# A decode kernel's first load ahead of its opening barrier, a semaphore barrier at its end, w_o of 28 heads in one transfer, and its output gathered to one partition

## Chip, cores and metric

The kernel runs on one core of a Trainium2 chip. The metric is the device time of one execution in microseconds (us). For every execution two numbers are recorded: this time, and the span, which goes from the first to the last instruction that the profile shows. For the difference of the two I write "time minus span". The record marks as fast every execution for which it lists a state, at mean granted TensorE clocks of 0.770 to 0.792.

## The reference, cut to what matters

One token is decoded (batch 1, width 512): layer norm, grouped-query attention with 32 query heads over 8 cached heads of 65536 keys each, output projection, residual, layer norm, a gated MLP of width 1792, residual. The two caches in bf16 are 268 of the 282 MB that are read.

```python
x = A_x
h = x + _A_ref(_layernorm(x), A_k_cache, A_v_cache, A_wq, A_wo)
#   softmax(q k^T * Dh**-0.5) v, then @ wo; q = (x @ wq), 32 heads of 128
h2 = h + _B_ref(_layernorm(h), B_w_gate, B_w_up, B_w_down)
#   (sigmoid(x @ w_gate) * (x @ w_up)) @ w_down
```

## The kernel before: the parts that matter here

The kernel streams the caches through a ring of four 4 MB slots with large transfers that SyncE (SP) issues. DVE transposes K, TensorE (PE) makes scores and value products. The program is five instruction streams, one for each engine, inside a block whose entry and exit are barriers of all engines:

```python
WO = ((0, 16), (16, 8), (24, 4), (28, 4))     # w_o: pieces of 16, 8, 4, 4 heads
WD_SPLIT = [(0, 7), (7, 12), (12, 14)]        # w_down: rows in three pieces
...
V_SPLIT = [(0, 3), (3, 4)]                    # the last V block in two pieces
W_SPLIT = {"wg": [(0, 4)], "wu": [(0, 3), (3, 4)]}
...
def regroup(i):                               # brings the heads' outputs into w_o's row order
    j0, n = WO[i]
    ...                                       # DVE product -> Lw[i]
    op("pe", lambda e: e.matmul(ps(OT[i], 0, n), lhsT=Lw[i][:, :], rhs=row_of[n][:, :], start=True, stop=True), ...)
    op("dve", lambda e: e.tensor_copy(O3[:, j0:j0 + n], ps(OT[i], 0, n)), ...)
...
for i, (nm, bank) in enumerate((("wg", GB), ("wu", UB))):
    ...                                       # 16 products for gate, 16 for up
    if i == 0:                                # the fp32 residual product, between the two
        op("pe", lambda e: e.matmul(ps(YB, 0, 128), lhsT=gsel[:, :], rhs=hz[:, :], start=True, stop=False, ...), ["hz"])
...                                           # tanh on ACT, product and transpose on DVE, 56 w_down products on PE
op("dve", lambda e: e.tensor_copy(y_sb[:, :], ps(YB, 0, 128)), ["y"], "ysb")
dma("sp", lambda e: e.dma_start(out[0].rearrange("o (g n) -> (o g) n", g=4),
                                bass.AP(tensor=y_sb, offset=0, ap=[[32 * 128, 4], [1, 128]])), "out", ["ysb"], "out")
op("sp", lambda e: None, ["out"])
block = es.enter_context(nc.Block("main"))
P.emit(block)
```

Of the kernel before, what the change touches and what calls it, by code (L numbers as in the profile page):

```python
# [14 lines left out]
GS = 4  # L15
# [20 lines left out]
class Prog:  # L36
# [3 lines left out]
    def __init__(self, nc, es):  # L40
        self.nc, self.es = nc, es
        self.ops = {e: [] for e in ("pe", "act", "dve", "pool", "sp")}
        self.where = {}
        self.alias = {}
        self.dma_sems = {}
        self.loop_sems = {}
        self.flow = {}
        self.part = {}

    def op(self, eng, fn, deps=(), name=None, to=None, times=1):  # L50
# [10 lines left out]

    def emit(self, block):
        for ops in self.ops.values():
            for o in ops:
                o["deps"] = [self.alias.get(d, d) for d in o["deps"]]
        needed = {d for ops in self.ops.values() for o in ops for d in o["deps"]}
        sems = {e: self.es.enter_context(self.nc.semaphore(f"s_{e}")) for e in self.ops}
# [122 lines left out]

        for e, deco in (("sp", block.sync), ("pool", block.gpsimd), ("act", block.scalar),
                        ("dve", block.vector), ("pe", block.tensor)):
            deco((lambda eng, e=e: hinted(e, eng)) if e in HINTED else (lambda eng, e=e: run(e, eng)))


def bass_sequential_preLN__gqa_block_cached__glu_gated_glu__decode_kernel(
# [13 lines left out]

    WO = ((0, 16), (16, 8), (24, 4), (28, 4))
    WD_SPLIT = [(0, 7), (7, 12), (12, 14)]
    FG = FF // 4

    with ExitStack() as es:
# [46 lines left out]
        hhT = sb("hhT", [128, FG], bf16)  # L262
        y_sb = sb("y_sb", [128, 128], bf16)

        W0 = NKT * CH
        O3 = sb("O3", [128, NQ], bf16)
        Lw = [sb(f"Lw{i}", [128, 128], bf16) for i in range(len(WO))]
        row_of = {n: sb(f"row_of{n}", [128, n], bf16) for n in (16, 8, 4)}
        blk_of = {n: sb(f"blk_of{n}", [128, 128 // n], bf16) for n in (16, 8, 4)}
        head_of = sb("head_of", [128, 4], fp32)  # L270
# [42 lines left out]
        V_SPLIT = [(0, 3), (3, 4)]  # L313
        W_SPLIT = {"wg": [(0, 4)], "wu": [(0, 3), (3, 4)]}
        W_AT = {"wg": 0, "wu": 4 * FF}
        for ld in order:
# [4 lines left out]
            if k == "wq":  # L321
                dma("sp", lambda e, d=dst: e.dma_start(d.rearrange("p (k n) -> p k n", k=4),
                    A_wq.rearrange("(p k) n -> p k n", p=128)), f"r{s}", deps, "wq")
            elif k in ("wg", "wu"):
                w = B_w_gate if k == "wg" else B_w_up
                dst, src = dst[:, W_AT[k]:W_AT[k] + 4 * FF], w.rearrange("(p k) n -> p (k n)", p=128)
                for i, (k0, k1) in enumerate(W_SPLIT[k]):
                    dma("sp", lambda e, d=dst, w=src, a=k0 * FF, z=k1 * FF: e.dma_start(d[:, a:z], w[:, a:z]),
                        f"{k}{i}", deps if i == 0 else (), f"{k}.{i}")
            elif k == "wd":  # L330
                src = B_w_down.rearrange("(p r) n -> p r n", p=128)
                for i, (r0, r1) in enumerate(WD_SPLIT):
                    dma("sp", lambda e, d2=dst[:, r0 * D:r1 * D].rearrange("p (r n) -> p r n", n=D), sr=src[:, r0:r1, :]:
                        e.dma_start(d2, sr), f"wd{i}", deps if i == 0 else (), f"wd{i}")
            else:
                h, r = b // NR, b % NR
                cache = A_k_cache if k == "K" else A_v_cache
                src = cache[0, h, r * BLK:(r + 1) * BLK, :].rearrange("(p t) d -> p (t d)", t=T)
                if ld == ("V", NB - 1):
                    for i, (c0, c1) in enumerate(V_SPLIT):  # L340
                        d2, s2 = (ap.rearrange("p (h c) -> p h c", h=2)[:, :, c0 * CH:c1 * CH] for ap in (dst, src))
                        dma("sp", lambda e, d2=d2, s2=s2: e.dma_start(d2, s2),
                            "v0" if i else "vl", deps if i == 0 else (), f"V{b}.{i}")
                else:
                    dma("sp", lambda e, d=dst, sr=src: e.dma_start(d, sr), f"v{s}" if k == "V" else f"k{s}" if k == "K" and b >= NR else f"r{s}",
                        deps, f"{k}{b}")
# [9 lines left out]
        for nm, t, v in (("onesf", onesf[:, :], 1.0), ("xz0", xz[:, :], 0.0), ("onef", one_f[:, :], 1.0), ("nhalf", nhalf[:, :], -0.5),  # L356
# [11 lines left out]
                                          bass.AP(tensor=head_of, offset=0, ap=[[4, 128], [0, 16], [1, 4], [0, 2]])), ["head"], "lsel")  # L368
        for n in (16, 8, 4):
            op("dve", lambda e, n=n: e.tensor_reduce(row_of[n][:, :], identf[:, :].rearrange("p (c r) -> p r c", r=n), AX.X, ALU.max),  # L370
               (), f"row{n}")
            op("dve", lambda e, n=n: e.tensor_reduce(blk_of[n][:, :], identf[:, :].rearrange("p (c r) -> p c r", r=n), AX.X, ALU.max),
               (), f"blk{n}")
        op("dve", lambda e: e.tensor_reduce(bass.AP(tensor=gsel, offset=0, ap=[[128, 128], [32, 4]]),
# [86 lines left out]

        op("pe", project_q, ["xz", "wq", "identf", "lsel", "onef", "sel", "gsel", "row4", "PTz", "qz0"], "q")
        op("act", lambda e: e.activation(  # L463
# [27 lines left out]
        def dve_block(b):  # L491
            s = slot_of[("K", b)]
            for c in range(NC):
                n = b * NC + c
                src = ring[:, s * SLOT + c * CH: s * SLOT + (c + 1) * CH].bitcast(fp32)
                dst = ktw[:, (n % NKT) * CH:(n % NKT + 1) * CH].bitcast(fp32)
                deps = [f"K{b}"] if c == 0 else []
                if b % NR or b == 0:
                    deps.append(f"S{b - 1}.{c}" if b else None)
                op("dve", lambda e, d=dst, sr=src: e.transpose(d, sr), deps, f"T{b}.{c}", to="T")  # L500
# [63 lines left out]
        def pv_regs(e):  # L564
            for half in range(NC // NR):
                for tq in range(4):
                    i = 8 * half + tq
                    if i:
                        e.reg_alu(reg(e, i), R["p"], 2 * (128 * tq + half), ALU.add)
                        e.reg_alu(reg(e, i + 4), R["v"], 2 * (half * NR * TC + 4 * tq) * 128, ALU.add)  # L570

# [26 lines left out]

        YT, STB, GB, UB, YB, OT = 0, MISC, 2, 3, 5, (1, 2, 3, 1)

        def regroup(i):

            j0, n = WO[i]
            op("dve", lambda e: e.tensor_tensor(Lw[i][:, :].rearrange("p (j c) -> p j c", j=n),  # L604
                                                bass.AP(tensor=O2, offset=j0, ap=[[NQ, 128], [1, n], [0, 128 // n]]),
                                                bass.AP(tensor=blk_of[n], offset=0, ap=[[128 // n, 128], [0, n], [1, 128 // n]]), ALU.mult),
               [f"o2.{(j0 + n) // GS - 1}", f"blk{n}"], f"Lw{i}")
            op("pe", lambda e: e.matmul(ps(OT[i], 0, n), lhsT=Lw[i][:, :], rhs=row_of[n][:, :], start=True, stop=True),  # L608
               [f"Lw{i}", f"PT{NB - 1}" if i == 0 else None], f"O3p{i}")
            op("dve", lambda e: e.tensor_copy(O3[:, j0:j0 + n], ps(OT[i], 0, n)), [f"O3p{i}"], f"O3.{i}")  # L610
# [10 lines left out]
        def project7():  # L621
            for i in range(3):
                regroup(i)
            waits = [d for i in range(3) for d in (f"O3.{i}", f"wo{i}")]
            def rows(e):
# [29 lines left out]
        def pe_flow(e, section):  # L655
# [50 lines left out]
            e.reg_alu(p, p, 2 * 512, ALU.add)  # L706
            e.reg_alu(v, v, 2 * CH, ALU.add)
            e.reg_alu(m, m, -1, ALU.add)
# [69 lines left out]
        P.part = {}  # L778
        regroup(3)
        project(range(NQ - GS, NQ), O3, ["O3.3", "wo3"], last=True)  # L780

# [10 lines left out]
        for i, (nm, bank) in enumerate((("wg", GB), ("wu", UB))):  # L792
            at = slot_of[(nm, 0)] * SLOT + W_AT[nm]
            for kt in range(4):
                for c in range(4):
# [5 lines left out]
                       ["hc"] * (kt == 0 and c == 0) + dep, f"gu{i}" if kt == 3 and c == 3 else None)  # L801
            if i == 0:
                op("pe", lambda e: e.matmul(ps(YB, 0, 128), lhsT=gsel[:, :], rhs=hz[:, :], start=True, stop=False, skip_group_check=True),  # L803
                   ["hz"])

# [7 lines left out]
        for i, (r0, r1) in enumerate(WD_SPLIT):  # L813
            for r in range(r0, r1):
                for g in range(4):
# [4 lines left out]
                       ["hhT", f"wd{i}"] if r == r0 and g == 0 else (), "y" if last else None)  # L820
        op("dve", lambda e: e.tensor_copy(y_sb[:, :], ps(YB, 0, 128)), ["y"], "ysb")  # L821
        dma("sp", lambda e: e.dma_start(out[0].rearrange("o (g n) -> (o g) n", g=4),
                                        bass.AP(tensor=y_sb, offset=0, ap=[[32 * 128, 4], [1, 128]])), "out", ["ysb"], "out")
        op("sp", lambda e: None, ["out"])

        block = es.enter_context(nc.Block("main"))
        P.emit(block)

# [27 lines left out]
```

## Time and profile before

| | before |
|---|---|
| time, median of the 6 executions of the first comparison | 663.33 us (662.69 to 663.78) |
| span of the profiled execution | 660.9 us |
| span, mean of the 31 executions beside my experiments | 661.2 us |
| moved from memory | 282.34 MB |
| first large packet, counted from the span's start | 1.74 us |
| last piece of w_down complete | 658.08 us |

Lines of the page of the kernel before: busy time of each engine and its share of the span, the granted TensorE clock and the busy share of the transfer engines in 40 slices (in tenths), the rate in each slice, then the transfer totals.

```profile
span 660.9 us, 6130 instructions
...
PE 424.1 (64%) x2316; PEld 73.6 (11%) x1548; DVE 350.5 (53%) x446; ACT 41.8 (6%) x111; POOL 3.6 (1%) x17
...
PEclk9899687677888697886966778766878758678576
DMA  9999999999999999999999999999999999999997
GB/s 381 440 418 438 434 426 440 420 438 434 424 440 424 434 438 420 440 424 436 436 420 440 432 428 438 420 438 434 426 440 419 438 434 426 440 422 421 435 421 320
DMA packets 11211, 282.34 MB, mean 427 GB/s; under 512 B 1225, under 2 KB 1226, under 8 KB 2250
...
q1 hardware_dynamic: 11208, 282.33, 99.5%
```

The row DMA says what bounds the kernel: the transfer engines are busy at 9 tenths or more in every slice but the last. PE, at 64%, waits for data. The packet records give the same more exactly: 431.7 to 431.9 GB/s in each 20 us window from 60 to 600 us, with 16.1 packets in flight on 16 engines.

The timeline of the kernel before at its start (start, length, engine or queue, line, operation):

```profile
0.73 0.51 ACTq L312 DMA_DIRECT2D x_row<-in_A_x_dram  x1
0.74 0.39 SPq L322 DMA_DIRECT2D ring<-in_A_wq_dram  x1
...
1.19 1.46 SPq L345 DMA_DIRECT2D ring<-in_A_k_cache_dram  x3
```

The kernel issues no transfer before 0.73 us; the opening barrier ends just ahead of that (its last record, on PE, ends at 0.72). At the other end, this is the chain of work that ended last in the kernel before (start, length, what):

```profile
651.77 1.66 PE PS L797 x12
653.44 0.73 PE PS L803 x2
654.16 1.43 PE PS L797 x15
...
655.62 0.92 DVE hh L809
...
656.57 0.66 DVE hhT L812
...
657.27 0.84 PE PS L817 x48
...
658.12 0.31 PE PS L817 x8
...
658.46 0.29 DVE y_sb L821
```

The timeline of the kernel before goes on from there with the write of the output:

```profile
658.77 0.66 SPq L822 DMA_DIRECT2D out_dram<-y_sb  x1
```

L797 are the gate and up products, L803 the residual product between them, L809 and L812 the DVE work on the MLP's hidden row, L817 the 56 products with w_down. The eight that start at 658.12 belong to the last piece of w_down, whose landing is recorded at 658.08: stream and compute end nearly together. The output write is issued at 658.77, lands at 660.45, and the closing barrier is through at 660.85.

### The profile page before, as it was taken

How to read it: one execution, taken by the hardware profiler on the slowest of the kernel's cores; microseconds unless marked ns; L12 is line 12 of the kernel's file. 1: busy time of each engine (PE TensorE's matmuls, PEld its weight loads, DVE VectorE, ACT ScalarE, POOL GpSimd, SP SyncE). 2: the span in 40 equal slices, each digit the busy share in tenths (PEclk: the TensorE clock that was granted, in tenths of full speed). 3: DMA queues.
4: the chain of work that ended last, by engine and by line, in shares of the span. 5: the costliest groups of instructions: out<-in, count | busy, mean ns of one | idle time of the engine just before them, and what ended most of it. 6: DMA issues, size and time to landing. Idle time of an engine off the chain costs nothing. (4 is left out here: it accounts for less than half of the span.)

```text
span 660.9 us, 6130 instructions
## 1 busy us (share of the span) xinstructions
PE 424.1 (64%) x2316; PEld 73.6 (11%) x1548; DVE 350.5 (53%) x446; ACT 41.8 (6%) x111; POOL 3.6 (1%) x17
## 2 busy tenths in 40 slices
PE   2797587548666585666765485764856668555855
PEld 1100010011000010010100110001100101001322
DVE  3598755547437655346555374465743565553102
ACT  0100200020000200020000200002000110002000
POOL 1000000000000000000000000000000000000000
PEclk9899687677888697886966778766878758678576
DMA  9999999999999999999999999999999999999997
GB/s 381 440 418 438 434 426 440 420 438 434 424 440 424 434 438 420 440 424 436 436 420 440 432 428 438 420 438 434 426 440 419 438 434 426 440 422 421 435 421 320
DMA packets 11211, 282.34 MB, mean 427 GB/s; under 512 B 1225, under 2 KB 1226, under 8 KB 2250
## 3 DMA queue, kind: packets, MB, share of 16 engines
q1 hardware_dynamic: 11208, 282.33, 99.5%
q14 instruction: 1, 0.01, 0.0%
q10 hardware_dynamic: 2, 0.00, 0.0%
HBM read 282.33 MB, written 0.00 MB: 427 GB/s over the span
## 5 line engine op out<-in xcount | busy, mean ns | idle before, releaser
L419 PE MATMUL PS<-ktw 128*128 128x512 bf16 x1024 | 304.2, 447 | 160.2 <-DVE ktw L500 156.5
L500 DVE STREAM_TRANSPOSE ktw<-ring 128x1024 f32<-128x1024 f32 x256 | 291.8, 1206 | 135.9 <-DMA ring<-in_A_k_cache_dram 135.8
L419 PE MATMUL PS<-ring,PT_sb 128*32 x1024 | 83.6, 456 | 23.7 <-issue 15.9
L419 PEld LDWEIGHTS PS<-ktw 128*128 x256 | 27.3, 107 | 415.1 <-issue 260.5
L554 DVE STREAM_TRANSPOSE PT_sb<-P_sb 128x512 bf16<-128x512 bf16 x32 | 20.1, 684 | 53.7 <-PE PS L591 52.2
L540 ACT ACTIVATE negmax<-PS 128x1 f32<-128x1 f32 x8 | 1.4, 171 | 527.2 <-PE PS L538 527.2
L419 PEld LDWEIGHTS PS<-ring,PT_sb 128*32 x1024 | 25.8, 116 | 79.5 <-issue 74.2
L505 DVE TENSOR_REDUCE M_sb<-PS 128x1 f32<-128x512 f32 x32 | 19.9, 682 | 25.1 <-PE PS L419 25.1
L544 ACT ACTIVATE P_sb<-PS,negmax 128x512 bf16<-128x512 f32 x32 | 21.5, 685 | 0.3
L561 DVE TENSOR_REDUCE lsum<-PS 128x1 f32<-128x4 f32 x8 | 1.3, 161 | 30.8 <-PE PS L559 30.8
L531 PE MATMUL PS<-identf,gm 128*1 128x128 f32 x16 | 3.1, 272 | 16.9 <-DVE gm L529 16.9
L604 DVE TENSOR_TENSOR Lw<-O,blk_of 128x128 bf16<-128x128 bf16 x4 | 1.1, 282 | 20.1 <-ACT O L595 20.1
L588 ACT ACTIVATE po_sb<-PS,rl 128x512 bf16<-128x512 f32 x8 | 5.5, 687 | 54.8 <-PE PS L419 54.8
L466 DVE STREAM_TRANSPOSE qt<-qh 32x512 bf16<-32x512 bf16 x1 | 0.7, 699 | 15.3 <-ACT qh L463 15.3
L419 PE MATMUL PS<-ring,xz 128*8 x32 | 8.6, 437 | 0.0
L419 PE MATMUL PS<-ktw,O 128*1 x26 | 8.5, 505 | 0.0
L538 PE MATMUL PS<-one_f,gmrep 1*128 1x1 f32 x16 | 3.8, 307 | 5.0 <-DVE gmrep L535 5.0
L544 ACT ACTIVATION_READ_ACCUMULATOR P_sb<-PS,negmax 128x1 f32 x32 | 6.5, 203 | 0.0
L591 PE MATMUL PS<-sel_bf,po_sb 128*128 128x4 bf16 x32 | 2.1, 169 | 6.3 <-ACT po_sb L588 6.3
L647 DVE TENSOR_TENSOR yr<-PS,x_row 1x512 f32<-1x512 f32 x1 | 0.7, 679 | 9.5 <-PE PS L645 9.5
L445 PE MATMUL PS<-qz 128*8 128x512 bf16 x2 | 1.0, 482 | 7.2 <-issue 7.2
L481 ACT ACTIVATE PS<-zcol 128x512 f32<-128x512 bf16 x8 | 5.0, 622 | 0.0
(81 smaller groups left out, 69.0 us busy)
## 6 DMA issues: line engine op xcount, KB each, us to landing
ring<-in_A_k_cache_dram SPq DMA_DIRECT2D x32, 4096.0 KB, 29.5
ring<-in_A_v_cache_dram SPq DMA_DIRECT2D x31, 4096.0 KB, 27.4
ring<-in_A_wq_dram SPq DMA_DIRECT2D x1, 4096.0 KB, 12.5
ring<-in_A_v_cache_dram SPq DMA_DIRECT2D x1, 3072.0 KB, 13.0
ktw<-in_A_wo_dram SPq DMA_DIRECT2D x1, 2048.0 KB, 9.9
ring<-in_B_w_gate_dram SPq DMA_DIRECT2D x1, 1792.0 KB, 18.5
ring<-in_B_w_up_dram SPq DMA_DIRECT2D x1, 1344.0 KB, 21.1
ktw<-in_A_wo_dram SPq DMA_DIRECT2D x1, 1024.0 KB, 12.0
```

What stands on the lines that cost most here:

```text
L419: return e.add_instruction(mybir.InstMatmult(name=nc.get_next_instruction_name(), engine=mybir.EngineType.PE, ins=[rhs, lhsT], outs=[e.low ...
L481: op("act", lambda e: e.activation(ps(PO, 0, 512), bass.AP(tensor=zcol, offset=0, ap=[[1, 128], [0, 512]]), AF.Copy), ["zcol"] if h == 0 e ...
L500: op("dve", lambda e, d=dst, sr=src: e.transpose(d, sr), deps, f"T{b}.{c}", to="T")
L505: op("dve", lambda e, u=u: e.tensor_reduce(M_sb[:, u % 4:u % 4 + 1], ps(u % NS, 0, 512), AX.X, ALU.max), [f"S{b}.{NC - NR + k}"], f"mx{u}" ...
L531: op("pe", lambda e: e.matmul(ps(MISC, 0, 128, 0, 1), lhsT=gm[:, :], rhs=identf[:, :], start=True, stop=True), [f"gm{h}"], f"gmT{h}", to="Q")
L538: op("pe", lambda e: e.matmul(ps(MISC, 128, 129), lhsT=gmrep[0:1, :], rhs=one_f[0:1, 0:1], start=True, stop=True), [f"gmrep{h}"], f"neg{h}")
L540: op("act", lambda e: e.activation(negmax[:, k:k + 1], ps(MISC, 128, 129), AF.Copy, scale=-att_scale), [f"neg{h}"], f"negmax{h}")
L544: op("act", lambda e, b=b: e.activation(P_sb[:, (b % 4) * 512:(b % 4 + 1) * 512], ps(b % NS, 0, 512), AF.Exp, bias=negmax[:, k:k + 1], sca ...
L554: op("dve", lambda e, b=b: e.transpose(PT_sb[:, (b % 4) * 512:(b % 4 + 1) * 512], P_sb[:, (b % 4) * 512:(b % 4 + 1) * 512]), [f"E{b}", f"o ...
L561: op("dve", lambda e: e.tensor_reduce(lsum[:, :], ps(MISC, 132, 136), AX.X, ALU.add), [f"l{h}"], f"ls{h}", to="D")
L588: op("act", lambda e: e.activation(po_sb[:, :], ps(PO, 0, 512), AF.Copy, scale=rl[:, :]), [f"PV{NR * h + NR - 1}", f"rl{h}"], f"po{h}", to ...
L591: op("pe", lambda e, t=t: e.matmul(ps(OX, 0, 4), lhsT=po_sb[:, t * 128:(t + 1) * 128], rhs=sel_bf[:, 8 * t:8 * t + 8:2], start=(t == 0), s ...
```

## The change

Its intent is to take out the microseconds at both ends that no transfer fills. The first load goes ahead of the opening barrier. The closing barrier uses semaphores alone, without draining each engine. Larger and fewer packets are used for w_o, w_up and the last V block, which becomes contiguous by another order of the chunks. The three pieces of w_down become 9, 4 and 1 of its rows, so that little work follows the last of them. The residual product moves behind the up product. Four small copies, two on DVE and two on ACT, gather the output in one partition, so that one packet of 1 KB is written instead of four of 256 bytes. The diff, cut to its core:

```diff
-    def emit(self, block):
+    def emit(self):
...
-        for e, deco in (("sp", block.sync), ("pool", block.gpsimd), ...):
-            deco(...)
+        nc, entry = self.nc, self.nc.cur_bb.bb
+        first = self.ops["sp"].pop(0)
+        assert first["dma"] and not first["deps"]
+        put("sp", nc.sync, first, [])
+        code = list(entry.instructions)
+        load = code.pop()
+        at = [i for i, ins in enumerate(code) if isinstance(ins, mybir.InstDrain) and ins.engine == mybir.EngineType.SP]
+        code.insert(at[0], load)
+        entry.instructions = code
+        for e, eng in (("sp", nc.sync), ...):
+            ...                                   # each engine's stream, then a branch to "fin"
+        nc.switch_bb("fin")
+        for sem, v, _ in (value[d] for d in self.at_end):
+            nc.sync.wait_ge(sem, v)
+        nc.all_engine_barrier(sem_only=True)
...
-    WO = ((0, 16), (16, 8), (24, 4), (28, 4))
-    WD_SPLIT = [(0, 7), (7, 12), (12, 14)]
+    WO = ((0, 28), (28, 4))
+    RW = 4
+    WD_SPLIT = [(0, 9), (9, 13), (13, 14)]
...
-        W_SPLIT = {"wg": [(0, 4)], "wu": [(0, 3), (3, 4)]}
+        W_SPLIT = {"wg": [(0, 4)], "wu": [(0, 4)]}
...
-                        d2, s2 = (ap.rearrange("p (h c) -> p h c", h=2)[:, :, c0 * CH:c1 * CH] for ap in (dst, src))
+                        d2, s2 = (ap[:, 2 * c0 * CH:2 * c1 * CH] for ap in (dst, src))
...
-            op("pe", lambda e: e.matmul(ps(OT[i], 0, n), lhsT=Lw[i][:, :], rhs=row_of[n][:, :], start=True, stop=True), ...)
+            for v in range(n // RW):              # 7 products for the 28 heads, in place of 3
+                lhsT = bass.AP(tensor=Lw[i], offset=v, ap=[[n * m, 128], [n // RW, 128]])
+                op("pe", lambda e, v=v, lhsT=lhsT: e.matmul(ps(OT[i], RW * v, RW * v + RW), lhsT=lhsT, rhs=row_of[:, :], ...), ...)
...
-            if i == 0:
-                op("pe", lambda e: e.matmul(ps(YB, 0, 128), lhsT=gsel[:, :], rhs=hz[:, :], ...), ["hz"])
+        op("pe", lambda e: e.matmul(ps(YB, 0, 128), lhsT=gsel[:, :], rhs=hz[:, :], ...), ["hz"])
...
-        op("dve", lambda e: e.tensor_copy(y_sb[:, :], ps(YB, 0, 128)), ["y"], "ysb")
-        dma("sp", ... four rows of 128 ...)
+        for g in (0, 2, 1, 3):                    # g < 2 on DVE, else on ACT
+            ...
+        dma("sp", lambda e: e.dma_start(out[0], y_sb[:, :]), "out", [f"ysb{g}" for g in range(4)], "out")
```

## The prediction

> **What bounds it now.** The transfer queue. In 20 us windows of the DMA packet records the 16 engines move 431.8 GB/s from 20 us to 600 us with 16.1 packets in flight, so no bubble is left; the page shows a DMA share of 9 tenths in all slices but the last. [...] PE (64%) and DVE (53%) wait for data. 282.34 MB are moved before and after. So only three places can give time: the start of the stream, its per-packet overhead, and what follows the last bytes.

> **Start.** The timeline has the first weight transfer issued at 0.74 us, after the opening barrier; its first packet starts at 1.74. Issued as SyncE's first instruction, it moves to about 0, and the whole stream with it: -0.7 us. The barrier and the layer norm come perhaps a little later, but that chain ends at 7.9 us and the weights land at 13.2, so there is slack; four removed DVE reductions (about 0.3 us each) help.

> **Packets.** Packet durations fit size/27 GB/s plus about 0.011 us. Merging w_o (512 to 256 packets), w_up (256 to 128) and the last V block made contiguous (512 to 256) removes 640 packets over 16 engines: -0.45 us. Stream end 657.66 becomes about 656.5.

> **Tail.** Chain of waits at the end: V piece 31.0 lands at 642.46 and PE starts at once; PE-paced from there (values, head output, regroup, projection, layer norm) to the gate product at 651.77. This shifts by about -1.0 (start plus w_o and V packets). Then:
> - The fp32 residual matmul (L803, 0.73 us between gate and up) moves behind up, under the DVE product and transpose (0.92 + 0.66): another -0.7, since w_up then lands at about 652.5, just in time.
> - So the hidden transpose is ready near 655.7 instead of 657.2, earlier than w_down. Now the stream binds: the last piece (one row instead of two) is seen at about 656.9, y is complete at 657.2 against 658.45: -1.25 in all, start and packets included.
> - Four 1x128 copies, two each on DVE and ACT: about 0.45 us against 0.29 for one: +0.15.
> - Output write, one packet of 1 KB instead of four of 256 B: issue to completion was 1.68 us; the load of x, also one packet of 1 KB, took 1.26. -0.3.
> - End: from the landing seen by SyncE (660.47) to the span's end 0.38 us, of which 0.16 us branch and drain go: -0.15.

> The 28-head regroup (a DVE product of about 1.1 us, estimated from 0.28 us for 128 columns, and seven matmuls against three round trips) replaces 2 us on PE at 616.5 to 618.5, where V transfers have some 4 us of slack: worth 0.

> **Sum.** -1.25 + 0.15 - 0.3 - 0.15 = -1.55 us. Predicted 661.9 us (before 663.49), range 661.1 to 663.1. Faster by over 2%: 0.01; within 2%: 0.98; slower: 0.01. Nothing here can reach 13 us.

> **What would show it.** Right: first 32 KB packet near 1.0 us; same rate in the middle; last w_down packet about 1.2 us earlier; PE waiting for w_down rather than for the DVE transpose; y copies 0.4 to 0.5 us; under 1.5 us from output issue to landing. Wrong: first packet still at 1.7 us; PE idle before up; the write as slow as before.

> **What would make it wrong.** SyncE's drain in the barrier may wait for the early transfer to finish, holding up the K transfers behind it and opening a gap of a microsecond or more; the queue may not take a transfer that early; the four copies may cost more than estimated, on ACT above all; w_up may land too late for the reordering to pay.

The fit of the packet durations is to the packet records of the kernel before: their means are 1.217 us for 32 KB, 0.614 for 16 KB, 0.163 for 4 KB, 0.085 for 2 KB and 0.009 for 4 bytes. The 0.45 us for the four copies is an estimate, for which the prediction gives no more than the 0.29 us of the one old copy. The 1.1 us for the regrouping product, also an estimate, came out at 1.07 in the trace after. Of the slack of some 4 us, the trace before shows that the last V transfers are issued at 629.46, 5.6 us before the one ahead of them lands (635.08).

## The result, and the profile after

| | before | after |
|---|---|---|
| time, median of 6 | 663.33 us | 662.30 us |
| lowest and highest time | 662.69 to 663.78 | 661.32 to 665.15 |
| span, mean | 661.2 us (31 executions) | 659.5 us (6 executions, 659.2 to 659.7) |
| time minus span | 1.8 to 2.2 us in 26 of 31, at most 3.3 | 2.08, 2.12, 2.13, 3.57, 5.44, 5.45 us |

The ratio of the times is 0.9995, with a 95% interval from 0.997 to 1.0019. (A ratio is the mean time of one kernel's fast runs over that of the other's of the same rounds, so not quite the ratio of the medians that I quote.) The median falls inside the predicted range. But the mean has hardly moved, and the times scatter over 3.8 us where the kernel before scatters over 1.1. The span is shorter in every execution, by 1.7 us in the mean. In three of the six executions something outside the span takes back 1.5 to 3.4 us, counted from 2.1.

First the span. The page after, in the lines that answer to those shown before:

```profile
span 659.6 us, 6128 instructions
...
DMA  9999999999999999999999999999999999999997
GB/s 400 427 443 417 443 431 427 441 417 445 427 431 433 425 443 417 443 429 429 435 423 445 423 435 433 425 439 419 445 429 429 433 425 443 423 437 421 437 422 325
DMA packets 10516, 282.34 MB, mean 428 GB/s; under 512 B 1170, under 2 KB 1300, under 8 KB 1556
...
q1 hardware_dynamic: 10514, 282.33, 99.6%
```

The transfer engines are as full as before, the bytes are the same, and 695 packets are gone (11211 less 10516). The first slice moves 400 GB/s instead of 381, which is the earlier start. The timeline after, at its start, shows that, and something that I had not expected:

```profile
0.00 0.41 SPq L342 DMA_DIRECT2D ring<-in_A_wq_dram  x1
...
0.80 0.51 ACTq L332 DMA_DIRECT2D x_row<-in_A_x_dram  x1
0.81 1.34 SPq L365 DMA_DIRECT2D ring<-in_A_k_cache_dram  x3
...
7.23 0.29 PE L419 MATMUL PS<-ident,x_row 1*128 1x1 bf16 x4 [7.23 <-DMA x_row<-in_A_x_dram]
```

SyncE's first instruction is now the load of w_q at 0.00. The packet records have its first packet at 1.04 us, against 1.74. SyncE's drain in the barrier took 0.12 us (from 0.46) and did not wait for the transfer, which landed at 12.30, so the K loads follow from 0.81. The little load of x is issued at 0.80 as before, but PE gets it only at 7.23 instead of 2.04: its packet started at 5.61 us, behind the packets of 32 KB that now fill the engines. In all 11 profiles with the early load it starts between 5.33 and 5.70 us; in the three with the load behind the barrier (before, r5_before_pad and r2_late_load below) it starts at 1.62 to 1.65. That it waits behind these packets is my reading. Its delay of 4.8 us (5.61 less 0.80) is as long as about four of them, at 1.2 us each in the trace. I did not test this further. The delay cost nothing visible, because the layer norm still ends (10.50 us) before w_q has landed (12.30).

The chain of work that ended last, after:

```profile
629.71 22.73 DMA ring<-in_B_w_up_dram
...
652.48 1.69 PE PS L818 x12
...
654.20 0.93 DVE hh L828
...
655.14 0.66 DVE hhT L831
...
655.84 1.69 PE PS L836 x42
```

The timeline after shows what the up products waited for:

```profile
652.48 1.66 PE L818 MATMUL PS<-ring,hc 128*1 128x448 bf16 x16 [0.35 <-DMA ring<-in_B_w_up_dram]
```

And the output's copies and its write:

```profile
657.56 0.56 ACT L844 ACTIVATE y_sb<-PS 1x128 bf16<-1x128 f32 x2 [4.73 <-PE PS L836]
657.56 0.59 DVE L842 CAST y_sb<-PS 1x128 bf16<-1x128 f32 x2 [1.77 <-PE PS L836]
658.21 0.33 SPq L846 DMA_DIRECT2D out_dram<-y_sb  x1
```

L818 are gate and up, L828 and L831 the DVE work, L836 the w_down products. The up products start at 652.48, when w_up lands; the residual product no longer stands ahead of them. PE stood idle for 0.35 us there, which is one of the signs that the prediction had named against itself ("PE idle before up"). Transposed activations are ready 1.4 us earlier than before (PE starts at 655.84, not 657.27). But the 56 products then took 1.66 us instead of 1.14, so the output copies begin at 657.56 rather than at the 657.2 that I forecast. The reason is in the windows view of just this stretch, first of the kernel before. Its columns are the stretch, its length, the busy time of PE, PEld, DVE, ACT and POOL with the number of instructions, then the granted clock, the busy share of the transfer engines and GB/s:

```profile
657.26:658.42 1.16, 1.12 (x56) 0.76 (x56) 0.00 (x0) 0.00 (x0) 0.00 (x0) 1.00 0.04 14
```

The same view after:

```profile
655.84:657.50 1.66, 1.66 (x56) 1.38 (x56) 0.00 (x0) 0.00 (x0) 0.00 (x0) 0.50 0.11 38
```

The granted clock is 1.00 in the first and 0.50 in the second: in the kernel before PE happened to have its full clock there, in the kernel after half of it. The last piece of w_down had landed at 656.82, so PE, not the stream, set the time at which the output was ready. Of my 14 profiles (these two and one of each experiment) 12 show 1.66 us for these products; only the kernel before with 1.14 and r9 with 1.24 are faster. In r9, at full clock, PE did wait for w_down as the prediction had it: the products of its last two pieces start at 656.80 and 657.12, just after the landings at 656.76 and 657.08. The windows view gives a granted clock of 1.00 for this stretch in r9, and of 0.50 in r10 (1.66 us). The duration changes from execution to execution, even for one kernel (1.66 us in r7 and 1.24 in r9, which are the same code). So the size of the clock effect is shown, and what sets the clock in the tail is not.

Now what lies outside. After the end of the span no instruction is recorded, but transfers are. These are the transfer queues after, from the end of the span to 666 us (packets, MB, share of 16 engines), of the execution shown above, whose time was 665.04 us:

```profile
q8 instruction: 1, 0.02, 1.3%
q14 instruction: 1, 0.01, 0.5%
```

One packet of 16 KB on queue 8, which the trace calls "instruction", started 2.4 us after the span had ended. I take it for a fetch of instructions. A second profile of the same kernel, of an execution that took only 661.62 us (r1_after_again below), has the packet too, but 1.5 us before the end, here in the window from 655 to 659.6 us:

```profile
q8 instruction: 1, 0.02, 1.9%
```

In the same stretches the kernel before has no such packet at all. So the question for the experiments was: what in the change brings this fetch, and is it what costs the time?

### The profile page after: what moved, and what is told of

Read it like the earlier page. It is cut to its first block, busy times and chain, and to the rows that moved or that the text cites. A ratio compares the mean times of both kernels' runs of the same rounds, so it can differ in the third digit from the quotient of the medians.

```text
span 659.6 us, 6128 instructions
## 1 busy us (share of the span) xinstructions
PE 425.5 (65%) x2320; PEld 74.4 (11%) x1552; DVE 349.8 (53%) x439; ACT 42.3 (6%) x113; POOL 3.6 (1%) x17
## 2 busy tenths in 40 slices
DMA packets 10516, 282.34 MB, mean 428 GB/s; under 512 B 1170, under 2 KB 1300, under 8 KB 1556
## 4 chain that ended last, share of the span: by engine, by line
DMA 39%; PE 28%; DVE 27%; issue 5%; ACT 1%; SPq 0%; DVEq 0%; POOL 0%
DMA ring<-in_A_k_cache_dram 34%; PE PS L436 25%; DVE ktw L518 20%; DMA ring<-in_B_w_up_dram 3%; DVE M_sb L523 3%; DVE PT_sb L572 2%; DMA x_row<-in_A_x_dram 1%; ACT po_sb L606 1%; PE PS L556 1%; PE PS L549 1%; DVE gmj L551 0%; DVE gmrep L553 0%; PE PS L609 0%; PE PS L836 0%; PE PS L818 0%
## 5 line engine op out<-in xcount | busy, mean ns | idle before, releaser
L623 DVE TENSOR_TENSOR Lw<-O,blk_of 128x896 bf16<-128x896 bf16 (+1 forms) x2 | 1.4, 683 | 20.6 <-ACT O L613 20.6
```

Source lines behind the costliest of these rows:

```text
L623: op("dve", lambda e: e.tensor_tensor(Lw[i][:, :].rearrange("p (j c) -> p j c", j=n), bass.AP(tensor=O2, offset=j0, ap=[[NQ, 128], [1, n], ...
```

## The experiments

| run | PE's stream, bytes | span, mean | time minus span, each execution | median time | ratio to before |
|---|---|---|---|---|---|
| before (31) | 31168 | 661.2 | 1.8 to 2.2 in 26; 2.3, 2.4, 2.9, 3.2, 3.3 | 663.2 to 663.3 | 1 |
| after (6) | 31616 | 659.5 | 5.4, 2.1, 5.5, 3.6, 2.1, 2.1 | 662.30 | 0.9995 |
| r1_after_again | 31616 | 659.5 | 2.1, 5.1, 5.6, 3.9, 2.1, 5.6 | 663.97 | 1.0008 |
| r2_late_load | 31616 | 660.2 | 2.0, 2.1, 5.4, 2.1, 5.8, 5.5 | 664.16 | 1.0013 |
| r3_drain_end | 31616 | 659.6 | 5.4, 2.1, 5.2, 2.1, 4.9, 4.2 | 664.17 | 0.9999 |
| r4_early_only | 31168 | 660.2 | 2.0, 2.5, 1.8, 1.8, 2.9 | 662.13 | 0.9986 |
| r5_before_pad | 32000 | 661.0 | 5.1, 5.4, 5.1, 5.0, 5.1 | 666.02 | 1.0041 |
| r6_after_pad320 | 52416 | 660.8 | 2.6, 1.8, 1.8, 1.8, 2.5 | 662.72 | 0.9990 |
| r7_four_wo | 31168 | 659.6 | 1.8, 1.8, 1.8, 1.8, 1.8 | 661.41 | 0.9972 |
| r8_old_output | 31616 | 659.7 | 5.4, 2.1, 5.4, 2.1, 2.1, 5.3 | 663.44 | 0.9996 |
| r9_four_wo_again | 31168 | 659.4 | 1.8, 1.8, 1.8, 1.9, 1.8 | 661.21 | 0.9970 |
| r10_hz_between | 31168 | 659.9 | 2.0, 1.8, 1.9, 3.3, 1.8 | 662.02 | 0.9982 |
| r11_three_wo | 31232 | 659.7 | 1.8, 1.8, 1.9, 1.8, 1.9 | 661.59 | 0.9976 |
| r12_after_pad64 | 36032 | 660.7 | 2.3, 1.9, 1.8, 2.4, 1.9 | 662.75 | 0.9991 |

All gave correct results. PE's lengths: the kernels with many long executions have 31616 or 32000, those without 31168, 31232, 36032 or 52416. The other four streams do not sort the kernels so: ACT's of 11712 bytes, POOL's of 4800 and SyncE's of 8320 stand in kernels with long executions and in kernels without, and DVE's are 13504, 13568 and 14144 in the first, 13696 to 14080 in the second.

### r1_after_again: the changed kernel, unedited

> The changed kernel, unedited. Its spans were 659.2 to 659.7 us in six runs, but its times 661.3 to 665.2, so what lies outside the span took 2.1 us in three runs, 3.6 in one and 5.4 in two; the one profile of the kernel before has 1.8. Theory A (the kernel's own end, or the layout of its code, causes it): the spread comes again, with spans near 659.5 and a time minus span that jumps between about 2 and over 3.5 us, while the kernel before stays within 0.5 us. Theory B (chance of that chip or hour): all times within 0.5 us of 661.5.

The scatter came again: four of six executions over 3.5 us outside the span, while the kernel before, in the same rounds on the same chip, stayed between 1.8 and 2.1 in ten of eleven executions and had one of 3.3. Chance of the hour (B) is out. My claim that the kernel before stays within 0.5 us was a little too strong.

### r2_late_load: the first transfer behind the barrier again

```diff
-        first = self.ops["sp"].pop(0)
-        ...
-        code.insert(at[0], load)
-        entry.instructions = code
```

> The changed kernel with the first transfer back behind the opening barrier. My account of the span: 0.7 us longer than the changed kernel, near 660.2 us, with the first large packet near 1.7 us. If the early transfer causes the long runs (rival C), time minus span stays near 2 us in all runs here; if the end does it (theory A), the jumps stay.

The span grew by 0.7 us (660.17 less 659.47), as predicted, and the first packet starts at 1.77 us. Three of six executions are still long, so the early transfer does not cause them (C is out).

### r3_drain_end: the full barrier at the end

```diff
-        nc.all_engine_barrier(sem_only=True)
+        nc.all_engine_barrier()
```

> The changed kernel with the full barrier (each engine drains first) at its end instead of the semaphore-only one. Theory A1 (the semaphore-only barrier lets something run late behind the span): no jumps, time minus span near 2 us, span about 0.05 to 0.15 us longer. Theory A2 (layout of the code) or C: jumps stay.

The long executions stay, four of six: A1 is out. The mean span is 0.13 us longer, as expected, but single spans of the changed kernel scatter over 0.5 us. In the profiles, from the landing of the output to the end of the span it takes 0.32 us here, 0.24 in the changed kernel and 0.40 in the kernel before.

### r4_early_only: the kernel before with the early transfer alone

```diff
+        first = self.ops["sp"].pop(0)
+        put("sp", nc.sync, first, [])
+        ...                                # moved ahead of SP's drain in the entry, as in the change
+        block = self.es.enter_context(nc.Block("main"))
```

> The kernel before with only the first transfer moved ahead of the barrier. My account: span 0.7 us shorter than the kernel before, near 660.2 us, the last w_down packet 0.7 us earlier. Rival: less than 0.3 us, if the tail is set by PE and not by the transfers. Rival C (the early transfer causes long runs): jumps of over 1.5 us in time minus span; theory A: none, about 1.8 us in all runs.

The span fell by 1.1 us (660.16 against 661.25 in the same rounds), the last piece of w_down landed at 657.09 instead of 658.08, and there are no jumps as large as those after. This part of the change is alone worth as much as the whole change in its median, and its ratio of 0.9986 (0.9973 to 0.9999) is below one, just. Why it gives 1.1 here and 0.7 in r2 is not settled: in its profile the slowest of the 16 transfer engines also lags less behind the fastest (about 0.5 us at the landings) than in the profile before (0.8 to 0.9 us, see under r6), and r5's profile shows that this lag varies between executions without the early transfer (0.44).

### r5_before_pad: the kernel before with a longer PE stream

```diff
             e.reg_mov(p, p0)
+            e.reg_mov(m, 1)
+            away("br_lt", m, 1, "unused", lambda: [e.matmul(...) for _ in range(4)])   # never taken
```

> The kernel before with 13 more instructions in PE's program, eight of them in a block that is never entered (PE's compiled program grows from 31168 to 32000 bytes; the changed kernel's has 31616). Theory D (the late 16 KB instruction fetch comes from the length of PE's program, which the change pushed over a boundary): spans as before, near 661.2 us, but the time minus span now jumps between about 2 and over 3.5 us as in the changed kernel, and a trace of a long run shows a 16 KB instruction packet on queue 8 after the span's end. Rival E (the new end of the program, or the early transfer, does it): time minus span stays near 2 us and there is no such packet.

This is the decisive run. It does the work of the kernel before, its span is that of the kernel before (661.0), and all five executions take 5.0 to 5.4 us outside the span. The packet is there behind the span's end too, in the queues from 661.2 to 666 us of this profile:

```profile
q8 instruction: 1, 0.02, 1.4%
```

Thirteen instructions in PE's stream, eight of which are never executed, cost 2.8 us of median time (666.02 less 663.22). Neither the early transfer nor the new end of the program is in this kernel, so E is out and D stands. I had expected jumps and got the long time in every execution; D in my form did not say which. (The build also lengthens the four other streams by two instructions each; r7, and the lengths given under the table, tell them apart.)

### r6_after_pad320: the boundary moved far forward

```diff
             e.reg_mov(p, p0)
+            e.reg_mov(m, 1)
+            away("br_lt", m, 1, "unused", lambda: [e.matmul(...) for _ in range(160)])  # never taken
```

> The changed kernel with a never entered block of 320 instructions ahead of PE's rarely used blocks (PE's program 52416 bytes), so that the boundary falls well ahead of the tail, into blocks that every head uses. Theory D: the 16 KB packet of queue 8 moves to the first heads, where PE has slack; time minus span is near 2.1 us in every run, spans near 659.5, so the median is near 661.6. Rival E: jumps as in the changed kernel. [...]

The jumps are gone: 1.8 to 2.6 us outside the span. The packets of 16 KB come at 23.8 and 66.4 us of the span, as forecast; one more came 1.9 us after the span, in an execution that took 2.55 us outside, so not every late packet is waited for. (Even if all of these 2.55 us lay behind the span, the execution was over 0.24 us before that packet ended.) But the span is 660.8 us, 1.3 more than the changed kernel's, which I had not foreseen. The landings say why. The trace records 16 landings for each of these transfers. I read them as one for each of the 16 transfer engines, which the trace does not name. The time between the first and the last of these sixteen, for the first nine transfers, with the time of the first landing of each (us):

```
first landing     11.7  21.4  31.1  40.8  50.6  60.3  70.0  79.7  89.4
after             0.58  0.57  0.57  0.58  0.59  0.59  0.58  0.59  0.59
r6_after_pad320   0.57  0.57  1.81  1.81  1.81  1.82  2.00  2.01  2.00
r12_after_pad64   0.59  0.56  0.55  0.56  0.58  0.58  1.77  1.77  1.76
before            0.90  0.88  0.87  0.86  0.87  0.85  0.85  0.86  0.88
```

(The first row is of the changed kernel; the padded ones agree to 0.2 us, the kernel before is up to 0.9 us later.) In r6 the lag of the slowest engine jumps by 1.2 us between the transfers that land at 21 and 31 us, around the fetch of 23.8, and rises once more, by only 0.2 us, after the one of 66.4. It is then still 1.99 us at the last piece of w_down. My reading is that the stream has no idle moment in which an engine could catch up (the page shows the transfer engines at 9 tenths or more in all slices but the last). The last landing is the one that counts: in the changed kernel those of w_up come from 651.88 to 652.44 us, and the up products, which wait for them, start at 652.48. The row of the kernel before shows that the lag with which the stream starts is kept too.

### r7_four_wo: w_o in four pieces, three regrouping products

```diff
-    WO = ((0, 28), (28, 4))
+    WO = ((0, 16), (16, 8), (24, 4), (28, 4))
```

(with the regrouping of the kernel before)

> The changed kernel with w_o in four pieces and three regrouping matmuls as before (PE's program 31168 bytes, as the kernel before). Theory D: no jumps, time minus span near 2 us, no packet on queue 8 behind the span. My account of the packets: 256 more packets of 4 to 16 KB cost 0.18 us of stream, so the span is 0.1 to 0.3 us over the changed kernel's. Rival E: jumps stay.

This shortens PE's stream to the 31168 bytes of the kernel before, and keeps all else of the change. The streams of DVE and SyncE get longer by eight and two instructions, the others stay, so PE's is the only one that shrinks. Every execution takes 1.8 us outside the span, and no packet on queue 8 is behind it. The time is 661.41 us, ratio 0.9972 (0.9959 to 0.9984): a little faster than the kernel before, and with a lower median than the changed kernel's 662.30, which was not timed in the same rounds.

### r8_old_output: the old copy and the old write

```diff
-        for g in (0, 2, 1, 3):
-            ...
-        dma("sp", lambda e: e.dma_start(out[0], y_sb[:, :]), ...)
+        op("dve", lambda e: e.tensor_copy(y_sb[:, :], ps(YB, 0, 128)), ["y"], "ysb")
+        dma("sp", ... four rows of 128 ...)
```

> The changed kernel with the old output: one copy of 128 partitions and a write of four packets of 256 bytes. From the two traces: the copy takes 0.30 us less (0.29 against 0.59), from its end to the landing 0.5 us more (1.68 against 1.12), so the span is 0.15 to 0.3 us over the changed kernel's. The jumps stay in theory D (PE's program has the same 31616 bytes) and in rival E.

The timeline of its tail, to be read beside that of the changed kernel:

```profile
657.56 0.29 DVE L840 CAST y_sb<-PS 128x128 bf16<-128x128 f32 x1 [1.77 <-PE PS L836]
657.88 0.65 SPq L841 DMA_DIRECT2D out_dram<-y_sb  x1
```

The write is issued 0.33 us earlier but lands later, at 659.54 instead of 659.33. The mean span is 0.2 us longer. The jumps stay, as they should with 31616 bytes.

### r9_four_wo_again: the base for the next runs

> The changed kernel with w_o in four pieces once more, as the base for the two runs beside it. Time near 661.4 us, time minus span 1.8 us in every run.

661.21 us, with 1.8 to 1.9 us outside in every execution. The two runs of this kernel have mean spans of 659.6 and 659.4 us against 659.5 of the changed one: the packets that merging w_o saves, forecast at 0.18 us, cannot be seen. Its profile does show a 16 KB packet on queue 8, 1.3 us before the end of the span, and the same kernel's profile in r7 shows none; so the fetch can be there without cost when it comes early enough. The short executions profiled in r1, r2 and r11 show the same: their packet starts 1.0 to 1.5 us before the span's end and has landed before it.

### r10_hz_between: the residual product between gate and up again

```diff
+            if i == 0:
+                op("pe", lambda e: e.matmul(ps(YB, 0, 128), lhsT=gsel[:, :], rhs=hz[:, :], ...), ["hz"])
-        op("pe", lambda e: e.matmul(ps(YB, 0, 128), lhsT=gsel[:, :], rhs=hz[:, :], ...), ["hz"])
```

> As r9, but the fp32 residual product is back between gate and up. My account in the prediction: the product costs 0.73 us there and the tail would gain that by moving it, so the span is 0.5 to 0.7 us longer than r9's if PE sets the pace of the tail. Rival: w_up lands only 0.3 us after the gate product ends, and w_down lands about 1 us after the transposed activations are ready, so transfers set the pace and the span is at most 0.2 us longer.

The mean span is 0.46 us longer than r9's (659.88 against 659.42), but only 0.24 longer than that of r7 (659.64), which has r9's code. So the gain is there, less than my 0.5 to 0.7 us, and the runs do not separate it well from the rival's 0.2. The timeline of this profile:

```profile
652.34 0.80 PE L823 MATMUL PS<-hz,gsel 128*128 128x128 f32 x2
...
653.06 1.66 PE L817 MATMUL PS<-ring,hc 128*1 128x448 bf16 x16
```

The up products start after the residual product, and w_up had landed 0.13 us before, at 652.93. In the changed kernel they start with the landing of w_up, after 0.35 us of waiting. So the product's 0.73 us are gained only as far as w_up lands early enough.

### r11_three_wo: w_o in pieces of 24, 4 and 4 heads

```diff
-    WO = ((0, 28), (28, 4))
-    RW = 4
+    WO = ((0, 24), (24, 4), (28, 4))
+    RW = (8, 4, 4)
```

(three regrouping products for the first piece, one for each other)

> As r9, but w_o in pieces of 24, 4 and 4 heads (128 packets fewer; PE's program 31232 bytes, between the 31168 that had no late fetch and the 31616 that had it). By my account of the packets the span is 0.05 to 0.1 us shorter than r9's. Theory D leaves open on which side of the boundary this length lies: time minus span is 1.8 in every run, or it jumps; a mean within 0.1 us of 1.8 puts the boundary above it.

Outside the span it takes 1.8 to 1.9 us, so by theory D the edge for this program lies between 31232 and 31616 bytes. The span did not shrink: 659.7 against 659.4 us. In its profile the w_down products took 1.66 us and in r9's 1.24, which is larger than the 0.05 to 0.1 us I was looking for; this run cannot resolve it.

### r12_after_pad64: the boundary moved by some 69 instructions

```diff
+            away("br_lt", m, 1, "unused", lambda: [e.matmul(...) for _ in range(32)])   # never taken
```

> The changed kernel with a never entered block of 64 instructions (PE's program 36032 bytes). The boundary then falls some 69 instructions earlier, among the last w_down products of PE. Theory D: time minus span is about 2 us in every run (the page is there before the program ends), and if the fetch is not begun ahead of need, PE stops among the products L836 plus offset [...]; if it is begun ahead, the span stays near 659.5. In both cases the 16 KB packet comes before the span's end.

No jumps, 1.8 to 2.4 us outside. The fetch came neither at the end nor ahead of the tail, but in the first head. The transfer queues from 60 to 70 us of this profile:

```profile
q1 hardware_dynamic: 150, 4.29, 99.9%
q8 instruction: 1, 0.02, 0.7%
```

This single packet started at 64.83 us and took 1.06 us. The lag of the slowest engine, in the table under r6, rises from 0.58 to 1.77 us between the transfers that land at 60 and 70 us, and the span is 1.2 us longer than the changed kernel's. So my picture of where the boundary lies was wrong, but a price of the fetch shows: here, in the middle of a full stream, it goes with a lag and a span that are longer by about its own length, as the first fetch of r6 does. (The second of r6 added only 0.2 us, so this is no fixed price.) PE did not stop among the w_down products: they took 1.66 us, as in the changed kernel. A second packet came 1.2 us behind the span, in an execution with 2.3 us outside.

## Why the prediction was right or wrong

The range (661.1 to 663.1 us) held the first median, and that is luck. Three of those six executions were short and three long, so the median of 662.30 lies in the gap between them; the same kernel timed again in r1 has a median of 663.97, outside the range. The forecast of the span was close, the step from the span to the time was wrong. Point by point:

- **What bounds the kernel: right.** The same rate and no bubbles after as before.
- **Start, -0.7 us: right.** First packet 1.04 us, forecast "near 1.0"; r2 puts the part at 0.7 us, r4 at 1.1.
- **Packets, -0.45 us: not shown.** 640 data packets did go, but the only part that I isolated, w_o at 0.18 us, is lost in the scatter of the spans (659.6 and 659.4 against 659.5).
- **The regrouping, "worth 0": right inside the span, wrong outside it.** Its four extra products lie in slack (the mean spans of r7 and r9, without them, are 659.6 and 659.4 us against 659.5), but their instructions lengthen PE's stream from 31168 to 31616 bytes. r7 and r9, which take them out, are the proof.
- **Residual product behind up, -0.7 us: right in kind, smaller.** r10: 0.46 us against r9, 0.24 against r7. w_up landed at 652.44 as forecast ("about 652.5"), but PE was ready for it 0.35 us earlier and stood idle.
- **"Now the stream binds ... y is complete at 657.2": wrong.** I took the 56 products at the 1.14 us that one profile before shows, at full clock. At half clock they take 1.66 us (granted clock 0.50 in the profiles after and of r10), and 12 of 14 profiles show that duration. PE never waited for w_down in the profile after; in r9, at full clock, it did, and the copies began at 657.40. The step that failed is the duration of these products.
- **Four copies, +0.15 us: too small.** They took 0.59 us against 0.29, so +0.30. **Output write, -0.3 us: too small as well.** Issue to landing fell from 1.68 to 1.12 us, so -0.56. The sum is about -0.26, and r8 measured 0.2 us.
- **Closing barrier, -0.15 us: right.** From landing to the span's end 0.40 us before and 0.24 after; r3's mean differs by 0.13 us.
- **Sum of the span, -1.55 us: close, in part by luck.** The mean spans give -1.7. The sum was built on the profile before, and the two profiles differ by only 1.3 (660.9 and 659.6): the w_down products at half clock took back half a microsecond that the forecast did not have, and the write gained more than it had. The profile before happened to have the full clock in its tail, and its span of 660.9 lies below the mean of 661.2.
- **From the span to the time: the step that failed.** The prediction read everything from the trace and took for granted that time minus span is a constant. It is nearly a constant, 1.8 to 2.2 us, for most executions of the kernel before; for the changed kernel and its three variants of the same PE length, 17 of 30 executions take 3.6 to 5.8 us. That takes back 1.4 us on average in the first comparison (a mean of 3.46 against 2.1) and 2.0 in r1, that is, about all of the gain.

What is shown: the length of PE's stream decides (r5 turns the kernel before slow with thirteen more instructions, r7 and r9 take seven away from the changed kernel and end its long executions), and a 16 KB instruction packet comes late in the profiles of the long executions of the changed kernel, of r3, r5 and r8. The 14 profiles sort without exception: in the four long executions (5.1 to 5.4 us outside) the packet starts 1.3 to 2.8 us after the span; in the eight of 1.8 to 2.1 us it lands before the span's end or does not come at all; r6 and r12 have their late packet after others that came early, and take 2.3 and 2.6 us. What is only argued: that an engine waits for this packet outside the span, in the instructions that follow the kernel. No instruction is recorded there. A hint: if all the time outside the span lies behind it, the long executions of the changed kernel, r3 and r8 end 1.7 to 1.8 us after their packet has ended, which is about what a short execution takes outside its span; but that of r5 ends 2.8 us after it. The late packets of r6 and r12 show that lateness alone is not enough. Why the fetch starts early in some executions of one kernel and late in others stays open, as do the few executions of about 3 us outside in the kernel before and in r10.

## What to carry to other kernels

Compare the time with the span for every execution, not only one: this change shortened the span by 1.7 us and lengthened, by up to 3.4 us in the first six executions, what the profile does not show. A time that scattered over 3.8 us, with spans within 0.5 us, was the sign of it here. When two versions of a program differ by a handful of instructions and by microseconds, test the length of the streams by itself, with instructions that never run. And in a tail of a few microseconds, read the clock beside each duration before you reuse it: one profile's 1.14 us at full clock were 1.66 us in most others.
